# Strassen's up product with one addition fewer, a wider accumulator bank, and a new table of dates

## The chip, the cores and the metric

The kernel runs on one core of a Trainium2 chip. The metric is the device time of one execution in microseconds, median over runs. A core has five engines with instruction streams of their own: PE (TensorE, matrix products; its weight loads are listed apart as PEld), DVE (VectorE), ACT (ScalarE), POOL (GpSimd) and SP (SyncE, which here issues most of the DMA transfers). Operands lie in SBUF; matrix products accumulate in the eight banks of PSUM, 2 KB for each of 128 partitions.

## The reference

```python
def _attn_ref(q, k, v, n_global, n_local):        # B 4, H 8, S 768, D 64; n_global 8, n_local 96
    scores = scale * np.matmul(q, k.transpose(0, 1, 3, 2))
    ...
    keep = is_global | is_local
    ...
    scores = scores + bias[None, :, :, :]          # ALiBi: -slope(head) * distance
    scores = np.where(keep, scores, -1000000000.0)
    ...
    return np.matmul(a, v)                         # a: softmax of scores over the keys

def _moe_ref(x, w_in, w_out):                      # x 3072 x 512, w_in 512 x 2048, w_out 2048 x 512
    h = x @ w_in
    g = h * (1.0 / (1.0 + np.exp(-1.702 * h)))
    return (g @ w_out).astype(np.float32)
```

The rows of the attention's result, all heads side by side, are the 3072 rows `x` of the second function.

## The kernel before

Every fp32 operand is split into two fp16 parts, high and low, and a product is made of three fp16 products. The attention works on 24 blocks of 128 rows (scores `s`, row maxima `NM`, exponentials `p`, values `pv`, result `x`, turned to `xT`). The second part works on 12 chunks `c` of 256 tokens. For each chunk the up product gives 2048 columns of `h`, then `g`, and the down product adds into `y`.

Chunks 0 to 2 use `up` (L861), a plain product. Chunks 3 to 11 use `up_two(c, S)`, S = 0..3, so 36 calls, each for 512 of the 2048 columns. A call is Strassen's algorithm in Winograd's form on 2x2 blocks: seven block products, in the order p1, p5, p6, p3, p2_, p7, p4, each of 12 matmuls of 128x128 (L901), on sums of weights (`T1` to `T4`) and of inputs (`xS`) that were made beforehand. They accumulate in two PSUM tiles, `pa` and `pb`:

- `pa` takes p1; ACT copies that (k1, L917) to `h0`; p6 is added on top, copied (k2, L906) to the other half of `h0`; p7 is added on top; DVE adds that to `h1` (q22); p4 is added on top.
- `pb` holds two sums: p5, copied to `h1` (k5, L906), with p3 on top, and p2_. DVE adds both to the halves of `h0` (q11 and q12, L909).

The sigmoid is made of a tanh: `swish` is one ACT tanh (L933) and one DVE product (L934). For the first half of a call, `h0` (512 wide), it runs once; for the second half it runs twice, over `h1` and over `pa`, 256 wide each. Then `g` is split, its high part on ACT (L941), its low part on DVE (L942), and `down_two` hands each half to `pile` (L969), which issues the down matmuls. For even S `pa` and `pb` are buffers of one ring of PSUM banks (`r_h`), for odd S each has a bank of its own.

The order of all instructions is fixed ahead: each step is a task with a cost, predecessors, buffers and a due time, and `order()` is a list scheduler that, engine by engine, takes the ready task with the earliest due time; the table `NUDGE` adds microseconds to the due times of all tasks with one tag. What comes out is one fixed program order for each engine; on the chip an engine waits for its next instruction and doesn't look past it.

The last tasks are a verdict on whether the fp16 parts hold the inputs: `rows_hold` (DVE), one small PE product `pb` (L1141) that sums over the partitions, `all_hold` (DVE, L1131 to L1137), which writes `flag`. Every engine loads `flag` into a register (L1159) and skips the fallback `general` when it is zero (L1160). Behind the skipped part stand only ACT's scaling of the last quarter of `y` (L994, `junk`) and the DMA of it that ACT issues (L998). ACT's two instructions wait for semaphore counts of DVE, PE and of the DMA queues; engines that skip `general` add to those counts by EVENT_SEMAPHORE instructions at the place they jump to.

Of the kernel before, what the change touches and what calls it, by code (L numbers as in the profile page):

```python
# [8 lines left out]
F32 = mybir.dt.float32  # L9
# [10 lines left out]
P = 128  # L20
# [6 lines left out]

NUDGE = {"M2": -8.8, "T2": 21.9, "T3": 11.2, "block1": 2, "block10u2": -2.7, "block10u2l": -0.5,  # L30
# [36 lines left out]

NG = 8
SKIP = 24
# [54 lines left out]
class Work:  # L124
# [5 lines left out]
    def add(self, on, fn, after=(), bufs=(), want=1e9):  # L130
        t = Task(on, fn, [a for a in after if a is not None], bufs, want)
        t.tag = self.tag + ("l" if "SP" in on else "")
        for a in t.after:
            a.next.append(t)
        for b in t.bufs:
            b.users.append(t)
        self.tasks.append(t)
        return t

    def order(self):  # L140
# [18 lines left out]
        for t in self.tasks:  # L159
            t.due += NUDGE.get(t.tag, 0.0)  # L160
        free = dict.fromkeys(("PE", "DVE", "ACT", "POOL", "SP"), 0.0)
# [84 lines left out]
def kernel(  # L246
# [11 lines left out]
    nc = tc.nc  # L258
# [70 lines left out]
    add = wk.add  # L329
# [68 lines left out]
    M1 = [add({"DVE": 0.61}, lambda e, f=f: slopes(e, slice(2, 3), range(4 * f, 4 * f + 4)), [m1], [mk]) for f in range(2)]  # L398
    wk.tag = "M2"
    m2 = add({"DVE": 0.78}, other, [m1], [flt, mk])  # L400
    M2 = [add({"DVE": 0.41, "ACT": 0.6}, lambda e, f=f: slopes(e, slice(0, 2), range(2 * f, 2 * f + 2)), [m2], [mk], 34.0) for f in range(4)]
# [475 lines left out]
    def up_two(c, S, want):  # L877


        nm = f"{c}_{S}"  # L880
        rx, rz = (r_h, r_h) if S % 2 == 0 else (r_y[1, 0], r_y[1, 1])
        pa, pb = Buf(rx, [P, 2, P], F32, "pa" + nm), Buf(rz, [P, 2, 2, P], F32, "pb" + nm)
        h0, h1 = Buf(r_VF, [P, 2, 2, P], F32, "h0" + nm), Buf(r_VF, [P, 2, P], F32, "h1" + nm)
        ts = [Buf(r_t, [P, 2, 2, P], F32, f"t{nm}_{t}") for t in range(2)]
        gg = [Buf(r_VR if t and c == NCHUNK - 1 else r_g, [P, 2, 2, 2, P], F16, f"g{nm}_{t}") for t in range(2)]
# [2 lines left out]
        half = lambda w, k: (w, lambda z: w()[:, z, 512 * k:512 * k + 512])  # L888
        (B11, B21), B22 = (half(W, 0), half(W, 1)), half(V, 1)
        (T1, T4), (T3, T2) = TT[S, 0], TT[S, 1]  # L890
        a, b, g_ = pa, (lambda: pb()[:, 0]), (lambda: pb()[:, 1])
        wr = [W_ready[2 * S, 0], W_ready[2 * S + 1, 0], x_ready[2 * c], x_ready[2 * c + 1]]
        tr = [*T_ready[S], xS_ready[c]]

# [10 lines left out]
        def keep(o, src, sb_, sp_, after):  # L905
            return add({"ACT": 0.26}, lambda e: nc.scalar.copy(o(), src()), after, [sb_, sp_])  # L906

        def plus(o, src, sb_, sp_, after):
            return add({"DVE": 0.34}, lambda e: nc.vector.tensor_add(o(), src(), o()), after, [sb_, sp_])  # L909

        c11, c12 = (lambda: h0()[:, 0]), (lambda: h0()[:, 1])
        p1 = product(a, B11, X, 0, 0, [*wr, line.get("p1")], pa, 0.0, first=True)
        p1.bufs.append(pb)
# [3 lines left out]
        k1 = add({"ACT": 0.26}, lambda e: nc.scalar.copy(c11(), a()), [p1, line.get("k1")], [h0, h1, pa])  # L917
        line["k1"] = k1
        k5 = keep(h1, b, h1, pb, [p5])
        p6 = product(a, T2, Xs, 0, 0, [*tr, k1], pa, 1.4)  # L920
        p3 = product(b, B22, Xs, 1, 0, [*tr, *wr, k5], pb, 2.1, last=True)
        p2_ = product(g_, B21, X, 1, 0, [*wr, p5], pb, 2.8, last=True)
        q11 = plus(c11, g_, h0, pb, [k1, p2_])
        k2 = keep(c12, a, h0, pa, [p6])
        q12 = plus(c12, b, h0, pb, [k2, p3])
        p7 = product(a, T3, Xs, 0, 1, [*tr, k2], pa, 4.1)
        q22 = plus(h1, a, h1, pa, [p7, k5])
        p4 = product(a, T4, X, 1, 1, [*tr, *wr, q22], pa, 5.5, last=True)
        ups[c, 2 * S] = ups[c, 2 * S + 1] = [p1, p5, p2_, p6, p3, p7, p4]

        def swish(o, src, srcs, after, w):

            t1 = add({"ACT": 0.06 + 0.22 * w}, lambda e: nc.scalar.activation(o(), src(), AF.Tanh, scale=0.851 / (SX * SW)), after, srcs)  # L933
            return add({"DVE": 0.08 + 0.265 * w}, lambda e: nc.vector.scalar_tensor_tensor(o(), o(), 1.0, src(), ALU.add, ALU.mult),  # L934
                       [t1], srcs)

        u0 = [swish(ts[0], h0, [ts[0], h0], [q11, q12], 2)]
        u1 = [swish(lambda: ts[1]()[:, 1], h1, [ts[1], h1], [q22], 1), swish(lambda: ts[1]()[:, 0], a, [ts[1], pa], [p4], 1)]
        for t, u in enumerate((u0, u1)):
            g, tt = gg[t], ts[t]  # L940
            t4 = add({"ACT": 0.53}, lambda e, g=g, tt=tt: nc.scalar.mul(g()[:, 0], tt(), SG / (SX * SW)), u, [tt, g])  # L941
# [76 lines left out]
    T0, PACE0, PACE, PACE2, LAG, SKEW, LEAD = 20.0, 6.0, 5.9, 5.7, 16.0, 3, 68.0  # L1018
# [67 lines left out]
    for s in range(NST):  # L1086
        for u in range(2):
            for half in range(2):
                ws = Buf(r_wa, [P, 512, 2], I32, f"ws{s}_{u}{half}again")
                t0 = add({"SP": 1.6}, lambda e, s=s, u=u, ws=ws, half=half: load_weights(nc, ws(), w_in, w_out, s, u, half), bufs=[ws])  # L1090
                o, hi_w = 2 * (2 * s + u) + half, lambda ws=ws: ws()[:, :, 1].bitcast(F32)
# [16 lines left out]
    pb = Buf(r_h, [P, 512], F32, "pb")  # L1108
# [255 lines left out]
```

## Time and profile before

| | us |
|---|---|
| median of 3 runs | 589.75 |
| the runs | 590.07, 588.32, 589.75 |
| profiled execution, its span | 587.0 |
| PE busy | 578.1 |
| DVE busy | 497.0 |
| ACT busy | 461.4 |

The profile shows one execution by its span, from its first instruction to its last; no other time of that execution is given, so what lies around the span is the 2.75 us between it and the median. "Busy" counts the time in which an engine executes an instruction. An engine's order is fixed, so an idle stretch on PE is a wait for another engine or for a transfer.

### The profile page before, as it was taken

What the parts mean: (1) busy time and instruction counts of PE and PEld (TensorE: products, weight loads), DVE (VectorE), ACT (ScalarE), POOL (GpSimd) and SP (SyncE); (2) the same over time, 40 slices, a digit from 0 to 9 for tenths busy, and PEclk for the clock granted to TensorE, in tenths of its full rate; (3) what the DMA queues carried; (4) which work ended last, traced back from release to release, by engine and by line L of the source; (5) the groups of instructions that cost most, each with busy time, mean ns of one, the idle gap of its engine ahead of it and who ended that gap; (6) DMA issues with size and microseconds to landing.
All of it is one profiled execution on the core that took longest, in us unless ns stands there. A gap on an engine that the chain in (4) does not pass through costs nothing.

```text
span 587.0 us, 16903 instructions
## 1 busy us (share of the span) xinstructions
PE 578.1 (98%) x6744; PEld 435.0 (74%) x6744; DVE 497.0 (85%) x1180; ACT 461.4 (79%) x1086; POOL 3.7 (1%) x14
## 2 busy tenths in 40 slices
PE   8999999999999999999999999999999999999996
PEld 5886666777678678778679767777777866876896
DVE  7898999999999999888899699889889878775462
ACT  6678899898678979888798798798987878874351
POOL 2000000000000000000000000000000000000000
PEclk9999999999999999999999999999999999999999
DMA  9988998988767887989999998999998899981101
GB/s 267 315 262 213 301 239 234 214 186 154 174 138 154 145 150 156 222 163 203 222 182 179 213 222 210 218 201 184 243 204 197 196 204 232 192 179 25 30 2 41
DMA packets 268265, 109.57 MB, mean 187 GB/s; under 512 B 249300, under 2 KB 249812, under 8 KB 268180
## 3 DMA queue, kind: packets, MB, share of 16 engines
q1 hardware_dynamic: 268032, 108.30, 83.3%
q8 instruction: 54, 0.88, 0.6%
q14 instruction: 31, 0.25, 0.1%
q10 hardware_dynamic: 148, 0.13, 0.1%
HBM read 57.67 MB, written 6.29 MB: 109 GB/s over the span
## 4 chain that ended last, share of the span: by engine, by line
PE 82%; DVE 6%; DMA 6%; ACT 4%; issue 2%; SPq 0%; POOL 0%; DVEq 0%; ACTq 0%; POOLq 0%
PE y L969 35%; PE pa L901 15%; PE pb L901 11%; PE h L861 7%; PE s L599 5%; DMA QKover<-qk16over 2%; PE pv L630 1%; PE pv L632 1%; PE pv L631 1%; PE sT L692 1%; DMA ws<-in_moe_w_out_dram 1%; DMA ws_00again<-in_moe_w_in_dram 1%; DMA xT<-x 1%; PE idle L1147 1%; PE pv L704 1%
## 5 line engine op out<-in xcount | busy, mean ns | idle before, releaser
L969 PE MATMUL y<-w,g 128*128 128x512 f16 (+1 forms) x1248 | 265.1, 363 | 0.3
L969 PEld LDWEIGHTS <-g 128*128 128x128 f16 x1248 | 118.0, 98 | 106.6 <-DVE g L873 1.4
L901 PEld LDWEIGHTS <-w 128*128 128x128 f16 x1728 | 101.4, 98 | 3.9
L615 ACT ACTIVATE p<-p,NM 128x232 f32<-128x232 f32 x160 | 76.3, 479 | 8.9 <-DVE NM L605 8.6
L901 PEld LDWEIGHTS <-T 128*128 128x128 f16 x1296 | 76.8, 98 | 5.2 <-issue 0.2
L861 PE MATMUL h<-xT,w 128*128 128x256 f16 x576 | 67.2, 273 | 0.2 <-DVE t L871 0.2
L605 DVE CUSTOM_DVE_ANT_0 p<-s,mm 128x232 f32<-128x232 f32 x160 | 57.5, 393 | 9.3 <-PE s L599 9.0
L861 PEld LDWEIGHTS <-w 128*128 128x128 f16 x576 | 55.4, 98 | 8.1 <-DVE t L871 0.3
L942 DVE SCALAR_TENSOR_TENSOR g<-t,g 128x512 f16<-128x512 f32 x72 | 49.0, 686 | 11.2 <-ACT g L941 10.9
L620 DVE TENSOR_TENSOR hl<-p,hl 128x464 f16<-128x464 f32 x80 | 50.8, 635 | 6.2 <-ACT hl L619 5.9
L941 ACT ACTIVATE g<-t 128x512 f16<-128x512 f32 x72 | 44.9, 628 | 12.1 <-PE y L969 8.2
L933 ACT ACTIVATE t<-h 128x512 f32<-128x512 f32 (+1 forms) x72 | 35.8, 517 | 17.8 <-DVE h L909 16.0
L619 ACT CAST hl<-p 128x464 f16<-128x464 f32 x80 | 46.0, 574 | 2.3 <-DMA pt<-hl 0.9
L909 DVE TENSOR_TENSOR h<-pb,h 128x256 f32<-128x256 f32 x72 | 28.4, 418 | 19.4 <-PE pb L901 17.8
L901 PE MATMUL pa<-xS,T 128*128 128x128 f16 x648 | 44.8, 219 | 0.0
L599 PEld LDWEIGHTS <-QK 128*128 128x128 f16 x640 | 36.5, 98 | 6.0 <-DVE NM L605 1.9
L934 DVE SCALAR_TENSOR_TENSOR t<-t,h 128x512 f32<-128x512 f32 (+1 forms) x72 | 38.4, 551 | 2.2 <-ACT t L933 2.0
L599 PE MATMUL s<-QK 128*128 128x128 f16 x320 | 38.2, 219 | 0.0
L901 PE MATMUL pa<-xT,w 128*128 128x128 f16 x540 | 37.5, 219 | 0.0
L901 PE MATMUL pb<-xS,w 128*128 128x128 f16 x540 | 37.5, 219 | 0.0
L632 PE MATMUL pv<-VR,pt 128*128 128x64 f16 x288 | 34.5, 193 | 0.0
L631 PE MATMUL pv<-VR,pt 128*128 128x64 f16 x288 | 34.5, 193 | 0.0
(186 smaller groups left out, 1031.2 us busy)
## 6 DMA issues: line engine op xcount, KB each, us to landing
ws<-in_moe_w_in_dram SPq DMA_DIRECT2D x8, 1024.0 KB
ws<-in_moe_w_out_dram SPq DMA_DIRECT2D x8, 1024.0 KB, 5.6
raw<-in_q_dram SPq DMA_DIRECT2D x24, 256.0 KB, 3.7
raw<-in_k_dram SPq DMA_DIRECT2D x24, 256.0 KB, 4.8
QK<-QK SPq DMA_DIRECT2D x40, 128.0 KB, 5.5
raw<-in_v_dram SPq DMA_DIRECT2D x20, 256.0 KB, 3.1
out_dram<-yo SPq DMA_DIRECT2D x20, 256.0 KB
ws_00again<-in_moe_w_in_dram SPq DMA_DIRECT2D x8, 512.0 KB, 4.0
```

What stands on the lines that cost most here:

```text
L599: nc.tensor.matmul(sp()[:, j, lo:hi], d["QK"]()[:, 0, h, :], K[:, 1 + z, h, P - (hi - lo):], start=(z == 0), stop=(z == 1), skip_group_che ...
L605: nc.vector.tensor_tensor_reduce(out=pr()[:, j, :], in0=sp()[:, j, :], in1=m, scale=-1.0 / SC, scalar=3.0e38, op0=ALU.add, op1=ALU.min, ac ...
L615: ex.append(add({"ACT": 0.473}, lambda e, j=j: nc.scalar.activation(pr()[:, j, :], pr()[:, j, :], AF.Exp, bias=NM[:, n, hs[j]:hs[j] + 1], ...
L619: t4 = add({"ACT": 0.5}, lambda e: nc.scalar.copy(hl()[:, 0, :, SKIP:], pr()), ex, [pr, hl])
L620: t5 = add({"DVE": 0.55}, lambda e: nc.vector.tensor_sub(hl()[:, 1, :, SKIP:], pr(), hl()[:, 0, :, SKIP:]), [t4], [pr, hl])
L631: nc.tensor.matmul(o, ph, V[:, 1, h], start=False, stop=False, skip_group_check=True)
L632: nc.tensor.matmul(o, pl, V[:, 0, h], start=False, stop=(s == ns - 1), skip_group_check=True)
L861: nc.tensor.matmul(ph()[:, fi, :], w1(s, cc, z, fi), X[:, y, cc, :], start=(j + cc == 0), stop=(j == 2 and cc == NCC - 1))
L901: nc.tensor.matmul(o()[:, fi], w, x()[:, y * NCC + 2 * k + cc, t], start=(first and fi + j + cc == 0), stop=(last and j + cc == 3), skip_g ...
L941: t4 = add({"ACT": 0.53}, lambda e, g=g, tt=tt: nc.scalar.mul(g()[:, 0], tt(), SG / (SX * SW)), u, [tt, g])
L942: t5 = add({"DVE": 0.61}, lambda e, g=g, tt=tt: nc.vector.scalar_tensor_tensor(g()[:, 1], tt(), SG / (SX * SW), g()[:, 0], ALU.mult, ALU.s ...
L969: nc.tensor.matmul(y(), part(zg, f), w2(s, z, f % 2)[:, m], start=(begin and f + j == 0), stop=(end and j == 2 and f == 2 * len(steps) - 1 ...
```

## The change

Four edits in `up_two`, and a new table.

- The tile `pa` is now a whole bank (2 x 256 columns) instead of half of one; products accumulate in its first half. The two halves of `pb` change places, so that they lie in the order of the halves of `h0`.
- q11 and q12, two additions of 256 columns, become one, q1, of 512; it waits for k1, k2, p2_ and p3.
- q22 writes its sum to the second half of `pa`, in PSUM, instead of to `h1`.
- For the second half of a call `swish` runs once, over all 512 columns of `pa`, after p4.
- `NUDGE` is replaced by a table with more entries, among them one for the verdict, which had none. Instructions of PE are the same in number and kind; DVE has 49 fewer, ACT 34 fewer: 36 additions, 36 products and 36 tanh are gone, and some other instructions change places between the two engines.

Lines of the changed kernel are 22 to 27 further on (L901 is L927, L969 is L991, L1141 is L1163, L1160 is L1182).

```diff
-NUDGE = {"M2": -8.8, "T2": 21.9, "T3": 11.2, "block1": 2, "block10u2": -2.7, "block10u2l": -0.5,
...
+         "up92": -40, "up93": -9.5, "verdict": 12.7, "w00": 14.7, "w00l": -2.4, "w01": -6.4, "w01l": -7.8,
...
-        pa, pb = Buf(rx, [P, 2, P], F32, "pa" + nm), Buf(rz, [P, 2, 2, P], F32, "pb" + nm)
+        pa, pb = Buf(rx, [P, 2, 2, P], F32, "pa" + nm), Buf(rz, [P, 2, 2, P], F32, "pb" + nm)
...
-        a, b, g_ = pa, (lambda: pb()[:, 0]), (lambda: pb()[:, 1])
+        a, b, g_ = (lambda: pa()[:, 0]), (lambda: pb()[:, 1]), (lambda: pb()[:, 0])
...
-        def plus(o, src, sb_, sp_, after):
-            return add({"DVE": 0.34}, lambda e: nc.vector.tensor_add(o(), src(), o()), after, [sb_, sp_])
...
-        q11 = plus(c11, g_, h0, pb, [k1, p2_])
         k2 = keep(c12, a, h0, pa, [p6])
-        q12 = plus(c12, b, h0, pb, [k2, p3])
+        q1 = add({"DVE": 0.62}, lambda e: nc.vector.tensor_add(h0(), pb(), h0()), [k1, k2, p2_, p3], [h0, pb])
         p7 = product(a, T3, Xs, 0, 1, [*tr, k2], pa, 4.1)
-        q22 = plus(h1, a, h1, pa, [p7, k5])
+        q22 = add({"DVE": 0.36}, lambda e: nc.vector.tensor_add(pa()[:, 1], a(), h1()), [p7, k5], [h1, pa])
...
-        u0 = [swish(ts[0], h0, [ts[0], h0], [q11, q12], 2)]
-        u1 = [swish(lambda: ts[1]()[:, 1], h1, [ts[1], h1], [q22], 1), swish(lambda: ts[1]()[:, 0], a, [ts[1], pa], [p4], 1)]
+        u0 = [swish(ts[0], h0, [ts[0], h0], [q1], 2)]
+        u1 = [swish(ts[1], pa, [ts[1], pa], [p4], 2)]
```

The instruction orders show the change at three places. The first is DVE in the call of chunk 6, S = 0 (names begin with `t6_0`, `h06_0`, `h16_0`, `pa6_0`), where `x14` and `sm2` belong to the attention of block 14. In the order of before:

```order
L909 TENSOR_TENSOR h16_0_5226<-pa6_0_5000,h16_0_5226 128x256
L942 SCALAR_TENSOR_TENSOR g5_3_1_5265<-t5_3_1_5163,g5_3_1_5265 128x512
L909 TENSOR_TENSOR h06_0_5144<-pb6_0_5130,h06_0_5144 128x256
L934 SCALAR_TENSOR_TENSOR t6_0_1_5324<-t6_0_1_5324,h16_0_5226 128x256
L747 TENSOR_SCALAR sm2_101<-sm2_101 128x8
L748 RECIPROCAL sm2_101<-sm2_101 128x8
L749 TENSOR_TENSOR x14_5354<-pv14_4959,sm2_101 128x512
L934 SCALAR_TENSOR_TENSOR t6_0_0_5350<-t6_0_0_5350,h06_0_5144 128x512
L934 SCALAR_TENSOR_TENSOR t6_0_1_5324<-t6_0_1_5324,pa6_0_5000 128x256
```

In the order of the change (`s15` and `p15` belong to the attention of block 15):

```order
L956 SCALAR_TENSOR_TENSOR t6_0_0_5284<-t6_0_0_5284,h06_0_5148 128x512
L631 ISA p15_2_5286,NM_89<-s15_2_5246,mm_102 128x232
L631 ISA NM_89 128x1
L956 SCALAR_TENSOR_TENSOR t6_0_1_5302<-t6_0_1_5302,pa6_0_5078 128x512
```

The two products of 256 columns for the second half have become one of 512, the last reader of the bank of `pa6_0`. The next call that takes this bank is chunk 6, S = 2. On PE, in the order of the change, these are the first and the last rows from p4 of the one (`pa6_0`) to p1 of the other (`pa6_2`), with the 32 matmuls between them cut to one of each product:

```order
L927 MATMUL pa6_0_5078<-xT6_4558,T0_1891 128x128
...
L927 MATMUL pb6_1_5288<-xS6_4981,T1_2262 128x128
...
L927 MATMUL pb6_1_5288<-xT6_4558,w2_0_581 128x128
...
L625 MATMUL s15_3_5321<-QK15_4775 128x128
...
L927 MATMUL pa6_2_5335<-xT6_4558,w4_0_817 128x128
```

Between them stand two products of 12 matmuls into `pb6_1` and eight score matmuls, the shortest such distance in the change.

The third place is the end of the program. PE in the order of before, where the verdict's product stands ahead of most of the last down products (`y11_00` is the first quarter of the last `y`, `y11_11` the last):

```order
L901 MATMUL pa11_3_9806<-xS11_9345,w5_0_942 128x128
L1141 MATMUL pb_9888<-fin_104,ones_110 1x3
L969 LDWEIGHTS g11_2_0_9775
L969 MATMUL y11_00_9497<-w4_1_846,g11_2_0_9775 128x256
```

and in the order of the change:

```order
L991 MATMUL y11_10_9524<-w7_1_1437,g11_3_1_9840 128x256
L1163 MATMUL pb_9885<-fin_104,ones_110 1x3
L991 LDWEIGHTS g11_1_1_9678
L991 MATMUL y11_11_9554<-w2_1_689,g11_1_1_9678 128x256
```

Behind the product there now stand only the 36 matmuls of `y11_11`. On DVE `all_hold` moves in the same way from ahead of the last five products of `t` and `g` to behind the last `yo`; on SP the load of `flag` moves from ahead of the last four `yo` transfers to behind them. SP before:

```order
L1159 TENSOR_LOAD flag [waits DVE_49]
L1159 ISA x2
L1002 DMA out_dram<-yo_0_9985 64x256 [waits DMAHW2_49,DVE_49]
L1002 DMA out_dram<-yo_0_9985 64x256 [waits DMAHW3_49]
L1002 DMA out_dram<-yo_0_9985 128x256 [waits DMAHW4_49,DVE_49]
L1002 DMA out_dram<-yo_1_10015 128x256 [waits DMAHW5_49,DVE_49]
L1160 COMPARE_AND_BRANCH
```

and in the change:

```order
L1024 DMA out_dram<-yo_0_9855 64x256 [waits DMAHW2_49,DVE_49]
L1024 DMA out_dram<-yo_0_9855 64x256 [waits DMAHW3_49]
L1024 DMA out_dram<-yo_0_9855 128x256 [waits DMAHW4_49,DVE_49]
L1024 DMA out_dram<-yo_1_9899 128x256 [waits DMAHW5_49,DVE_49]
L1181 TENSOR_LOAD flag [waits DVE_49]
L1181 ISA x2
L1182 COMPARE_AND_BRANCH
```

The branch now follows the load with only the two ISA rows between.

## Rows read from the trace of the kernel before

**Rows 1.** The page: span, busy time of each engine with its share of the span and its instructions, and the granted clock of PE in 40 slices (9 is 90% or more of full speed).

```profile
span 587.0 us, 16903 instructions
PE 578.1 (98%) x6744; PEld 435.0 (74%) x6744; DVE 497.0 (85%) x1180; ACT 461.4 (79%) x1086; POOL 3.7 (1%) x14
PEclk9999999999999999999999999999999999999999
```

**Rows 2.** Busy time by stretch: start:end and length in us, then busy us and instructions of PE, PEld, DVE, ACT and POOL, the granted clock, the DMA share and GB/s.

```profile
20.00:60.00 40.00, 38.90 (x329) 31.39 (x328) 35.65 (x59) 30.42 (x41) 0.00 (x0) 1.00 0.90 265
60.00:140.00 80.00, 78.99 (x737) 56.24 (x736) 77.75 (x159) 73.11 (x152) 0.00 (x0) 1.00 0.97 234
140.00:220.00 80.00, 80.00 (x918) 58.10 (x914) 78.04 (x178) 64.41 (x154) 0.00 (x0) 1.00 0.73 147
220.00:300.00 80.00, 80.00 (x1046) 60.19 (x1044) 68.49 (x174) 68.10 (x175) 0.00 (x0) 1.00 0.91 191
420.00:460.00 40.00, 39.86 (x508) 29.43 (x506) 34.01 (x83) 33.77 (x88) 0.00 (x0) 1.00 0.98 200
```

**Rows 3.** Timeline of PE from 402 to 408 us: start, duration of the run from first start to last end, engine, line, operation, names, shapes and count.

```profile
402.36 0.83 PE L901 MATMUL pa<-xT,w 128*128 128x128 f16 x12
403.03 2.75 PE L969 MATMUL y<-w,g 128*128 128x512 f16 x12
...
407.31 0.26 PE L599 MATMUL s<-QKover,QK 128*128 128x104 f16 x2
...
407.71 0.83 PE L901 MATMUL pb<-xS,w 128*128 128x128 f16 x12
```

**Rows 4.** Waits of PE's weight loads over the whole span: line and what it waited for, us in total, times, longest.

```profile
PEld L599 <- DVE NM L605: 1.9, 3, 1.0
PEld L969 <- DVE g L873: 1.4, 3, 0.6
PEld L969 <- DVE g L942: 0.6, 1, 0.6
```

**Rows 5.** Groups of instructions by line and shape: line, engine, operation, output<-inputs, shapes and count, then busy us in all and mean ns of one, then idle time before them. `pa`, `pb` and `pv` lie in PSUM, the rest in SBUF.

```profile
L909 DVE TENSOR_TENSOR h<-pb,h 128x256 f32<-128x256 f32 x72 | 28.4, 418 | 19.4 <-PE pb L901 17.8 <-ACT h L906 0.8 <-ACT p L615 0.4
L934 DVE SCALAR_TENSOR_TENSOR t<-t,h 128x512 f32<-128x512 f32 x36 | 24.6, 684 | 2.2 <-ACT t L933 2.0
L933 ACT ACTIVATE t<-h 128x512 f32<-128x512 f32 x36 | 22.6, 627 | 13.3 <-DVE h L909 12.1 <-DMA out_dram<-yo 1.1
L909 DVE TENSOR_TENSOR h<-pa,h 128x256 f32<-128x256 f32 x36 | 15.0, 418 | 0.8 <-PE pa L901 0.6
L934 DVE SCALAR_TENSOR_TENSOR t<-t,h 128x256 f32<-128x256 f32 x36 | 15.0, 417 | 0.0
L934 DVE SCALAR_TENSOR_TENSOR t<-t,pa 128x256 f32<-128x256 f32 x36 | 14.9, 415 | 5.5 <-ACT t L933 5.5
L933 ACT ACTIVATE t<-h 128x256 f32<-128x256 f32 x36 | 14.6, 407 | 4.5 <-DVE h L909 4.0 <-DVE g L942 0.4
L749 DVE TENSOR_TENSOR x<-pv,sm 128x512 f32<-128x512 f32 x20 | 13.8, 692 | 3.9 <-PE pv L632 1.6 <-DVE sm L748 0.5
L933 ACT ACTIVATE t<-pa 128x256 f32<-128x256 f32 x36 | 13.6, 377 | 7.1 <-PE pa L901 7.1
```

**Rows 6.** Weight loads of `up_two`'s products over the whole span: line, engine, operation and count, then ns shortest/median/longest, then first and last start in us.

```profile
L901 PEld LDWEIGHTS <-w x1728: 95/98/98, 173.8 to 571.8; 128*128 128x128 f16 x192
```

**Rows 7.** The chain that ended last, from 560 us on: start, us, engine, output, line and count.

```profile
569.84 0.12 PE pb L1141 x2
...
572.05 10.49 PE y L969 x96
...
582.62 0.47 ACT junk L994
```

**Rows 8.** Timeline of DVE from 569 us on, columns as in the timeline of PE.

```profile
570.28 0.14 DVE L1131 COPY tot<-pb 1x3 f32<-1x3 f32 x1
...
571.42 0.14 DVE L1137 TENSOR_SCALAR flag<-tot 1x1 int32<-1x1 f32 x1
...
578.64 0.42 DVE L985 TENSOR_SCALAR yo<-y 128x256 f32<-128x256 f32 x1 [0.89 <-PE y L969]
```

**Rows 9.** The instructions of L1159 (load of the flag), L1160 (branch, and the semaphore steps behind it) and L998 (the last DMA): engine queue, operation and count, then ns shortest/median/longest, then first and last start in us.

```profile
L1159 SPq TENSOR_LOAD <-flag x1: 477/477/477, 571.6 to 571.6; - x1
L1159 DVEq TENSOR_LOAD <-flag x1: 542/542/542, 578.6 to 578.6; - x1
L1160 SPq EVENT_SEMAPHORE  x8: 17/17/17, 582.2 to 582.8; - x8
L1160 ACTq COMPARE_BRANCH  x1: 45/45/45, 573.5 to 573.5; - x1
L1160 ACTq EVENT_SEMAPHORE  x1: 17/17/17, 573.9 to 573.9; - x1
L1160 DVEq COMPARE_BRANCH  x1: 72/72/72, 579.3 to 579.3; - x1
L1160 SPq COMPARE_BRANCH  x1: 58/58/58, 579.5 to 579.5; - x1
L1160 DVEq EVENT_SEMAPHORE  x1: 21/21/21, 582.2 to 582.2; - x1
L998 ACTq DMA_DIRECT2D out_dram<-junk x1: 376/376/376, 583.1 to 583.1; - x1
```

More of the change, by code (lines that the diff above doesn't have):

```diff
@@ L26 @@
 LOW = 1e8
-NUDGE = {"M2": -8.8, "T2": 21.9, "T3": 11.2, "block1": 2, "block10u2": -2.7, "block10u2l": -0.5,
[36 rows of a table removed]
+NUDGE = {"M1": -24.1, "M2": -17.9, "T0": -7.8, "T1": 6.4, "T3": 11.6, "again": 14.4, "againl": 1.4,
[62 rows of a table added]
 NG = 8
```

97 rows, old and new, of the table NUDGE are left out of this document.

## The prediction, made before the changed kernel ran

> **What bounds the kernel now.** I read the page first. [...] The share is an average, so the stretches come next [rows 2]. From 140 us on PE is busy 80.00 of 80 us twice, then 39.86 of 40 in the worst of the later ones; DVE in the same stretches is busy 98%, 86% and 85%. There the end is set by PE's work alone. Earlier it is different: from 20 to 60 us PE lacks 1.10 us, from 60 to 140 us 1.01 us, and in the latter DVE is busy 77.75 of 80 us.
>
> Busy PE need not be PE at its best pace, so the timeline has to show the spacing [rows 3]: a product of 12 matmuls starts at 402.36 and the next thing at 403.03, 0.67 us; eight score matmuls take 407.71 - 407.31 = 0.40 us. Seven products take 4.69 us for PE, a call's whole share, and I find that spacing nearly everywhere after 130 us. Last, the waits of PE's weight loads [rows 4]: 1.9 us on the row maxima NM, 1.4 and 0.6 us on the low part of g, all from DVE. These few microseconds, and the end of the program, are all that a change off PE can win or lose.
>
> **What is removed.** A call of `up_two` loses work on two engines and none on PE. On DVE two additions at 418 ns become one of 512 columns [rows 5]. No row has that operation between PSUM and SBUF; the nearest are the normalisation of x, the same operation from PSUM at 512 columns, 692 ns, and the product of 512 columns, 684 ns. With 0.69 us a call saves 0.15 us, 36 calls 5.3 us. The two products of the second half, 417 + 415 ns, become one of 684 ns: 0.15 us, 5.3 us in all. On ACT the tanh of 407 + 377 ns become one of 627 ns: 0.16 us, 5.7 us in all. The times of one instruction overlap a little from one to the next, so DVE gains somewhat less, say 8 us. The first weight load of `up_two` is at 173.8 us [rows 6], so all of it falls behind the stretch in which PE waits; the cover is PE's own full row of work [rows 2], and the 8 us are worth nothing there by themselves.
>
> **What is changed in place.** q22 writes PSUM instead of SBUF. No row shows DVE writing to PSUM. Below, 0 extra: reading `pb` or `pa` instead of SBUF leaves products at 415 beside 417 ns [rows 5]. Above, 0.1 us for each (the 274 ns by which 692 exceeds 418 are twice the columns, not the place, so I find no row for more): 36 x 0.1 = 3.6 us of DVE time, covered from 220 us on by 14% of idle DVE. I take 0.
>
> **What is added: a longer hold on the bank.** Before, q22's half could pass tanh and product while PE did p4; only 377 + 415 ns of work over `pa` remained behind p4. Now all 512 columns wait for p4, 627 + 684 ns, 0.52 us more before the bank is free and before `g` can be split. For the split it matters little: the down products that need this half stand far enough behind p4 in the new order. For the bank it may matter. [...] The shortest distance on PE is that of chunk 6 shown in the change: two products and eight score matmuls, 2 x 0.67 + 0.40 = 1.74 us [rows 3]. Ahead of the last product DVE has there the product for the first half (684 ns) and a row maximum. So this place is at its limit: 0 to 1 us of wait. Counting PE's work in the new order at the same spacings I find two more under 3 us, 2.4 and 2.8. Bounds 0 and 2 us together; I take 0.3, since the nominal chain fits at the shortest place, and most others have over 4 us.
>
> [...]
>
> **New dates, front.** PE's order in the first 54 us is nearly the old one, with a few neighbours exchanged; its waits for ACT and DVE there should stay: 0, with 0.3 either way.
>
> **New dates, 60 to 140 us.** Here DVE is 97% busy and PE waits for it [rows 2]. Laying DVE's work ahead of each wait against PE's, in both orders, at the durations of before, DVE's worst lag behind PE's pace shrinks by 0.5 to 1 us. The waits that could go are those of [rows 4], 1.9 + 1.4 + 0.6 us as weight loads see them, and 1.0 us as PE sees them in 60 to 140 us [rows 2], since loads run ahead of products. I take 0.7 us of gain, bounds 0 and 1.2. In the later stretches PE lacks little, 0.14 us in the row from 420 us; I take 0.1 of gain.
>
> **New dates, the verdict.** This is the largest single term. Before, PE's verdict product stands at 569.84 [rows 7], `all_hold` runs from 570.28 to 571.56 on DVE, 1.28 us [rows 8], and SP loads the flag at 571.6 [rows 9], eleven microseconds ahead of the end of PE at 572.05 + 10.49 = 582.54. Now the product stands ahead of the last 36 matmuls. A down matmul of 256 columns takes 10.49 / 96 = 0.109 us [rows 7], so 36 of them take 3.93 us, and `y11_10` ends at 578.6, as the last `yo` at 578.64 confirms [rows 8]. `yo` ends at 579.0, `all_hold` starts with it done and takes 1.28 us: flag at 580.2 to 580.3. SP's load takes 0.48 us and some register work; I put its branch at 581.0.
>
> What follows the branch decides. On SP the branch is at 579.5 and the eight semaphore steps at its target start at 582.2 and end at 582.8: 2.7 + 0.6 us. On DVE it is at 579.3, the step at 582.2: 2.9 us. On ACT it is 573.5 to 573.9: 0.4 us [rows 9]. With SP's time again: 581.0 + 2.7 + 0.6 = 584.3. With DVE's: load at 580.2, branch 0.7 us later as before, step at 583.8, and then ACT's scaling (474 ns) until 584.3. ACT's last DMA waits for both, and it stands now at 583.1 [rows 9]; nothing hides the difference, since that DMA ends the span 3.9 us later. So +1.2 us. Bounds: 0, if both engines go on as quickly as ACT did (SP 581.0 + 0.4 + 0.6 = 582.0, before PE ends), and +1.5 with the latest reading of each step. I take 1.2: the rows for the two engines in question are the near ones.
>
> [...]
>
> **The sum**, against the span of the profiled execution: 587.0 + 1.2 (verdict) + 0.3 (bank) - 0.7 - 0.1 (waits) = 587.7 us, +0.7. The median of before lies 2.75 us above that span, so 589.75 + 0.7 gives 590.4 us.
>
> **Rivals.**
>
> *The verdict is hidden, and the waits go* (faster). If SP and DVE find the code behind the branch as ACT did, the 1.2 us vanish. Then 0.3 - 0.8 = -0.5 gives 589.2. For it to be faster by more than the measurement can tell, 0.3% or 1.8 us, all 1.2 us of the waits and the 1.1 us that PE lacks in 20 to 60 us must go: -2.3 gives 587.4 us. Against: both engines that matter took nearly 3 us in the trace. Chance of faster than that bound: 0.17.
>
> *The bank is late* (slower). If the first product of a call waits for `pa` at the three short places, and at some others because DVE has an attention row ahead, PE loses 2 us more than I took, and the verdict's 1.2 us remain: 590.4 + 2.0 = 592.4. It decides from the point where the hand-over behind p4 takes over 1.74 us at chunk 6, or over 2.4 us at the next place. [...] Against: most places have over 4 us. Chance 0.15.
>
> *The new dates are worse early.* DVE at 97% has no reserve, so a row maximum put two instructions later (0.7 us each) costs PE as much; three such places are +2 us, again 592.4. Against: the lag that I work out is smaller. Chance 0.06.
>
> *Nothing measurable happens*, the edits lying off the bound and the dates cancelling: my own case, with its 0.7 us unseen.
>
> **How the numbers follow.** My case and its neighbours within 1.8 us of 589.75 have 0.62. Slower by more: 0.15 + 0.06 = 0.21. Faster: 0.17. My own case lies between 589.0 (no verdict term) and 591.4 (the bank at 1.4). For 8 in 10 the range reaches half-way into the rivals: 588.2 to 592.2.
>
> **What would show it.** DVE's busy time should fall to 487 to 490 us and ACT's by some 5 us plus or minus what changes places, with PE's at 578 as before. The 512-column addition should read 0.68 to 0.70 us; q22 0.42. PE's busy share in 60 to 140 us should reach 79.5 of 80. At the end, SP's first semaphore step should stand over 2 us behind its branch, and ACT's DMA over a microsecond behind the end of PE's last product. I am wrong if PE waits for DVE's product over `pa` at chunk 6 or elsewhere by more than 1 us, if ACT's DMA follows PE's end as closely as before (0.6 us), or if DVE's saving reaches PE after all because waits that the trace books as busy PE disappear.

## The result, and the profile after

The changed kernel takes 591.61 us (median of 5 runs, 591.02 to 592.86); the kernel before took 589.74 us in the runs beside it (5 runs, 588.32 to 590.07). The ratio is 1.0054, with a 95% interval of 1.0035 to 1.0074: slower by 3.2 us by the ratio over runs taken in turns; the two medians stand 1.87 us (0.32%) apart, just under the lower end of the interval. The prediction was 590.4 us, no change that a measurement can tell. The time lies inside its range, but the kernel is slower by more than the noise, and that was not forecast.

The profiled execution took 592.86 us with a span of 591.1 us, so 1.76 us lie around the span. In the five runs of the change that figure is 1.75 to 1.9 us. Span and median of before stood 2.75 us apart; the profiled execution of before was therefore about a microsecond quicker than its median, and the 4.1 us between the two spans are more than the difference of the kernels.

The page of the changed kernel, its first lines (as [rows 1]):

```profile
span 591.1 us, 16801 instructions
PE 578.5 (98%) x6744; PEld 435.4 (74%) x6744; DVE 493.3 (83%) x1107; ACT 454.5 (77%) x1051; POOL 3.7 (1%) x14
```

DVE is 3.7 us less busy and ACT 6.9 us, PE is as busy as before in a longer span. Busy time by stretch (as [rows 2]):

```profile
60.00:140.00 80.00, 77.60 (x722) 55.12 (x720) 76.92 (x157) 71.06 (x149) 0.00 (x0) 1.00 0.97 230
...
300.00:380.00 80.00, 78.74 (x1056) 60.05 (x1054) 67.45 (x159) 65.47 (x168) 0.00 (x0) 1.00 0.98 194
```

PE lacks 2.40 us from 60 to 140 us (80.00 less the busy 77.60), where it lacked 1.01, and 1.26 us from 300 to 380 us, where before it lacked nothing in this execution. What PE waited for (engine, line, cause: us, times, longest):

```profile
PE h L887 <- DVE t L897: 1.4, 2, 0.7
PE s L625 <- DVE NM L631: 1.0, 1, 1.0
PE aux L706 <- DVE top L703: 0.9, 1, 0.9
PE pv L656 <- DMA pt<-hl: 0.6, 1, 0.6
PE pa L927 <- ACT h L932: 0.4, 1, 0.4
```

The first two are in the early stretch, the third at 10 us; the last two are those near 312 and 341 us. The joined instructions themselves (columns as in [rows 5]):

```profile
L947 DVE TENSOR_TENSOR h<-pb,h 128x512 f32<-128x512 f32 x36 | 24.7, 686 | 13.1 <-PE pb L927 9.5 <-ACT h L932 3.3
L956 DVE SCALAR_TENSOR_TENSOR t<-t,pa 128x512 f32<-128x512 f32 x36 | 24.5, 681 | 1.8 <-ACT t L955 1.7
L955 ACT ACTIVATE t<-pa 128x512 f32<-128x512 f32 x36 | 21.3, 592 | 13.7 <-PE pa L927 11.6 <-DVE sm L773 2.1
L949 DVE TENSOR_TENSOR pa<-pa,h 128x256 f32<-128x256 f32 x36 | 15.4, 426 | 6.5 <-PE pa L927 6.4
```

The addition of 512 columns takes 686 ns, the one that writes PSUM 426 ns against 418.

The end of the program. PE and then DVE on the timeline (as [rows 8]):

```profile
581.35 0.19 PE L1163 MATMUL pb<-fin,ones 128*1 128x3 f32 x2
581.47 4.10 PE L991 MATMUL y<-w,g 128*128 128x256 f16 x36
...
582.93 0.14 DVE L1159 TENSOR_SCALAR flag<-tot 1x1 int32<-1x1 f32 x1
```

and the flag's load, the branch, the semaphore steps behind it and ACT's last two instructions (as [rows 9]):

```profile
L1181 SPq TENSOR_LOAD <-flag x1: 478/478/478, 583.1 to 583.1; - x1
L1182 SPq EVENT_SEMAPHORE  x8: 17/17/17, 587.4 to 587.9; - x8
L1182 DVEq COMPARE_BRANCH  x1: 72/72/72, 583.7 to 583.7; - x1
L1182 SPq COMPARE_BRANCH  x1: 58/58/58, 584.3 to 584.3; - x1
L1182 DVEq EVENT_SEMAPHORE  x1: 21/21/21, 584.3 to 584.3; - x1
L1016 ACT ACTIVATE junk<-y,room x1: 473/473/473, 585.7 to 585.7; 128x256 f32<-128x256 f32 x1
L1020 ACTq DMA_DIRECT2D out_dram<-junk x1: 376/376/376, 588.1 to 588.1; - x1
```

PE's last product ends at 585.57. ACT's scaling follows at once, at 585.7, but its DMA starts at 588.1, behind SP's eight steps (587.4 to 587.9). Before, the DMA stood 0.6 us behind PE's end, now 2.5. The end of the span moved less: it lies 5.4 us behind the start of ACT's scaling (591.1 and 585.7), before 4.4 (587.0 and 582.62 [rows 7]), because the last transfer ended the span 3.0 us after its issue and not 3.9.

### The profile page after: what moved, and what is told of

It reads as the page before. It is cut to its first block, busy times and chain, and to the rows that moved or that the text cites. A ratio compares the mean times of both kernels' runs of the same rounds, so it can differ in the third digit from the quotient of the medians.

```text
span 591.1 us, 16801 instructions
## 1 busy us (share of the span) xinstructions
PE 578.5 (98%) x6744; PEld 435.4 (74%) x6744; DVE 493.3 (83%) x1107; ACT 454.5 (77%) x1051; POOL 3.7 (1%) x14
## 5 line engine op out<-in xcount | busy, mean ns | idle before, releaser
L991 PE MATMUL y<-w,g 128*128 128x512 f16 (+1 forms) x1248 | 264.3, 363 | 0.0
L991 PEld LDWEIGHTS <-g 128*128 128x128 f16 x1248 | 118.2, 98 | 107.3 <-DVE g L899 0.5
L927 PEld LDWEIGHTS <-w 128*128 128x128 f16 x1728 | 101.1, 98 | 3.4 <-issue 0.3
L927 PEld LDWEIGHTS <-T 128*128 128x128 f16 x1296 | 76.6, 98 | 3.9 <-issue 0.5
L927 PE MATMUL pa<-xS,T 128*128 128x128 f16 x648 | 45.0, 219 | 0.4 <-ACT h L932 0.4
L927 PE MATMUL pb<-xS,w 128*128 128x128 f16 x540 | 37.3, 219 | 0.2 <-ACT h L932 0.2
L927 PE MATMUL pa<-xT,w 128*128 128x128 f16 x540 | 36.8, 219 | 0.0
L947 DVE TENSOR_TENSOR h<-pb,h 128x512 f32<-128x512 f32 x36 | 24.7, 686 | 13.1 <-PE pb L927 9.5
L657 PE MATMUL pv<-VR,pt 128*128 128x64 f16 x288 | 34.8, 193 | 0.0
L658 PE MATMUL pv<-VR,pt 128*128 128x64 f16 x288 | 34.8, 193 | 0.0
L656 PE MATMUL pv<-VR,pt 128*128 128x64 f16 x288 | 34.8, 193 | 0.0
L484 ACT ACTIVATE junk<-raw 128x1024 bf16<-128x1024 f32 (+1 forms) x40 | 33.6, 839 | 0.6 <-issue 0.4
```

The costliest lines, as they stand in the source:

```text
L656: nc.tensor.matmul(o, ph, V[:, 0, h], start=(s == 0), stop=False, skip_group_check=True)
L657: nc.tensor.matmul(o, ph, V[:, 1, h], start=False, stop=False, skip_group_check=True)
L927: nc.tensor.matmul(o()[:, fi], w, x()[:, y * NCC + 2 * k + cc, t], start=(first and fi + j + cc == 0), stop=(last and j + cc == 3), skip_g ...
L991: nc.tensor.matmul(y(), part(zg, f), w2(s, z, f % 2)[:, m], start=(begin and f + j == 0), stop=(end and j == 2 and f == 2 * len(steps) - 1 ...
```

## The experiments

Each is given as a ratio to the kernel before, timed on the same chip in turns with it. Theory 1 is that the late verdict costs, theory 2 that PE's waits from the new dates cost, theory 3 that the edits themselves cost, by the longer hold on the bank of `pa`. Two more came up on the way.

**The verdict of the change, dated earlier.**

```diff
-         "verdict": 12.7,
+         "verdict": 4,
```

> The changed kernel with its verdict dated 8.7 us earlier, so that the flag is written and SP loads it ahead of the last yo transfers; all else as in the change. If the late verdict is a cost (theory 1): ACT's last DMA follows PE's last product by 0.6 us again instead of 2.5, the time falls by 1.0 to 2.0 us, to 589.6 to 590.6. If the cost is only PE's waits from 60 to 380 us (theory 2): within 0.4 us of 591.6.

Measured: 589.59 us beside 588.11 of before, ratio 1.0023 (1.0012 to 1.0033). Against 1.0054 this is 0.31%, 1.8 us; by the two intervals it can be 0.5 to 3.1 us. In its trace, the chain's last pieces, then SP's branch and steps and ACT's DMA:

```profile
574.97 10.17 PE y L991 x93
...
585.21 0.47 ACT junk L1016
```

```profile
L1182 SPq EVENT_SEMAPHORE  x8: 17/17/17, 585.0 to 585.5; - x8
L1182 SPq COMPARE_BRANCH  x1: 58/58/58, 582.4 to 582.4; - x1
L1020 ACTq DMA_DIRECT2D out_dram<-junk x1: 376/376/376, 585.7 to 585.7; - x1
```

SP's branch comes 2.8 us ahead of ACT's scaling and its steps are through in time; the DMA stands 0.6 us behind PE's end again. The span ends 4.0 us behind the start of the scaling, 1.4 us less than in the change. The late verdict is a cost, theory 1 holds for it, but 0.23% are left. The same kernel was run once more on another chip:

> The changed kernel with the early verdict once more, beside the two others on one chip: 1.0012 to 1.0033 of before, as the first time.

Measured: 589.52 beside 587.89, ratio 1.0023 (1.0013 to 1.0033).

**The verdict of before, dated later.**

```diff
-         "x9l": 1.9}
+         "x9l": 1.9, "verdict": 20}
```

> The kernel before with its verdict dated 20 us later, so that the flag is written behind the last yo; all else as before. Theory 1: ACT's last DMA stands 2 to 2.5 us behind PE's end, the time rises by 1.0 to 2.0 us, to 590.8 to 591.7. Theory 2: 589.7, unchanged within 0.4.

Measured: 591.41 us, ratio 1.0058 (1.0044 to 1.0073), 3.4 us, more than any theory had. Here both engines are slow behind the branch:

```profile
L1160 SPq EVENT_SEMAPHORE  x8: 17/17/17, 585.0 to 585.6; - x8
L1160 DVEq COMPARE_BRANCH  x1: 72/72/72, 581.2 to 581.2; - x1
L1160 SPq COMPARE_BRANCH  x1: 58/58/58, 581.4 to 581.4; - x1
L1160 DVEq EVENT_SEMAPHORE  x1: 21/21/21, 585.0 to 585.0; - x1
L998 ACTq DMA_DIRECT2D out_dram<-junk x1: 376/376/376, 585.7 to 585.7; - x1
```

DVE takes 3.8 us and SP 3.6, and since DVE is late ACT's scaling is late too (585.1, with PE done at 581.7).

**The edits with the dates of before.** The body of the change, the old table; the order is made anew.

```diff
-NUDGE = {"M1": -24.1, "M2": -17.9, "T0": -7.8, ...
+NUDGE = {"M2": -8.8, "T2": 21.9, "T3": 11.2, ...
```

> The four edits in up_two alone, with the dates of before (the verdict early). If the edits cost nothing (theories 1 and 2): 589.2 to 590.2, PE's waits ahead of 140 us as before. If the longer hold on the bank of pa costs (theory 3): 591 or more, with PE waits for DVE's product over pa or for ACT's tanh in 220 to 560 us.

Measured: 591.39 us, ratio 1.0053 (1.0040 to 1.0067). By its expectation that speaks for theory 3, but the trace shows another cause. ACT, then PE, near 306 us:

```profile
305.30 0.68 ACT L1088 ACTIVATE ws_00again<-ws_00again 128x512 f32<-128x512 f32 x1 [2.88 <-DMA ws_00again<-in_moe_w_in_dram]
...
307.52 0.37 ACT L906 COPY h<-pa 128x256 f32<-128x256 f32 x1
```

```profile
307.94 0.83 PE L901 MATMUL pa<-xS,w 128*128 128x128 f16 x12 [1.28 <-ACT h L906]
```

ACT stands 2.88 us at a check of reloaded weights, whose transfer is late. In the order made with the old dates this check stands ahead of the copy that PE's next product needs; in the trace of before the copy stands at 304.78, ahead of the same check. PE has other waits in this execution: 0.9 us for transposed p, 0.7 us for values, 0.5 us for a copy that had too little work between itself and the next product. None is for the product or the tanh over `pa`.

**The dates of the change with the old body.** The new table in the kernel before.

```diff
-NUDGE = {"M2": -8.8, "T2": 21.9, "T3": 11.2, ...
+NUDGE = {"M1": -24.1, "M2": -17.9, "T0": -7.8, ...
```

> The table of the change alone, with up_two as before. If the dates are the whole difference (theories 1 and 2): 591.2 to 592.4, with PE losing about 1.5 us at the row maxima near 72 us and at the up products near 107 and 111 us, and the late verdict's tail. If the edits in up_two are the difference (theory 3): 589.3 to 590.3.

Measured: 602.05 us, ratio 1.0235 (1.0216 to 1.0255). Neither theory has this. PE's largest waits:

```profile
PE pa L927 <- ACT h L943: 3.1, 2, 2.3
PE pb L927 <- DVE xS L823: 1.5, 1, 1.5
```

Copies and sums come too late for PE, as in the run before this; what holds each of them up was not followed further. In the early stretch the trace has the wait of the change: 1.4 us for `t` (L897), here with the old body. A table and a body belong together; neither alone is a measure of what it adds to the other. Here, besides, ACT jumps slowly and SP quickly:

```profile
L1186 SPq EVENT_SEMAPHORE  x8: 17/17/17, 590.4 to 590.9; - x8
L1186 ACTq COMPARE_BRANCH  x1: 50/50/50, 589.5 to 589.5; - x1
L1186 SPq COMPARE_BRANCH  x1: 58/58/58, 589.8 to 589.8; - x1
L1186 ACTq EVENT_SEMAPHORE  x1: 17/17/17, 592.8 to 592.8; - x1
```

**Theory 4: ACT's wait for the reloads.** Three kernels in exactly the orders of before, of the edits with old dates, and of the change with the early verdict; only the operand of the 32 checks is another, and with it the places that they write.

```diff
-                o, hi_w = 2 * (2 * s + u) + half, lambda ws=ws: ws()[:, :, 1].bitcast(F32)
+                o, hi_w = 2 * (2 * s + u) + half, lambda: idle
...
```

> The kernel before, in its own order, but the 32 checks of the reloaded weights (ACT square, DVE minimum) read a tile that is always there instead of the one that the DMA brings; the reloads stay, the check of the weights' range is left out. If ACT's wait for these reloads is what the edits made costly (theory 4), before has little of it: 0 to 0.4 us under before (587.7 to 588.1 on this chip). A rival, that the reloads' traffic or the checks' work cost by themselves, would also give no change here; it is told apart by the next run.

> The four edits with the dates of before, in the same order as in body_only, with the checks reading the resident tile as in the run before this. Theory 4: ACT no longer stands 2.9 us at the reload near 302 us, PE's wait of 1.4 us for a copy near 306 us is gone, the time falls by 1.2 to 2.2 us from 591.4. Rival (the edits' longer chain on the bank and on ACT costs, theory 3): within 0.5 us of 591.4. Waits of PE for transposed p and for VR (0.9 and 0.7 us) may stay in either.

> The changed kernel with the early verdict, in the same order, with the checks reading the resident tile. Theory 4: PE's waits near 341 to 379 us, 1.2 to 2 us, go or halve; the time falls by 0.6 to 1.5 us from 589.6. Rival (theory 3): within 0.4 us of 589.6.

Measured: before 589.40 us beside 588.82, ratio 1.0006 (0.9991 to 1.0020), no change; the edits with old dates 590.81, 1.0039 (1.0023 to 1.0056), 0.14% under the 1.0053 of that kernel; the change with the early verdict 590.88, 1.0042 (1.0026 to 1.0057), over its 1.0023. Neither difference is clear of the intervals. In the traces the wait at 306 us is gone, and PE's waits behind 150 us are few: in the change with the early verdict a single one of 0.2 us, in the edits with old dates these:

```profile
PE pv L630 <- DMA VR<-VG: 0.8, 1, 0.8
PE pa L901 <- ACT h L906: 0.5, 1, 0.5
```

But the times didn't follow as forecast. The program's end hides a part. With the edits and old dates ACT's scaling starts at 584.5 and not 586.3, 1.7 us earlier, and then the last transfer takes 1.0 us of that back: it ends the span 4.3 us after its issue and not 3.3. In the change with the early verdict it takes 4.7 us where it took 3.5 and 3.4. These are single executions. So the mechanism at 306 us is seen, its worth in the time is not settled; for the change as it is, theory 4 isn't borne out.

**Theory 5: the edits in the old order.** The joined instructions stand where the later of the two stood, nothing is scheduled anew.

```diff
+        joined.append((q11, q12, lambda e: nc.vector.tensor_add(h0(), pb(), h0()), None))
...
-        for t in wk.order():
+        seq_ = wk.order()
+        when = {t: i for i, t in enumerate(seq_)}
+        for x, z, fn, made in joined:
+            first_, last_ = sorted((x, z), key=lambda t: when[t])
+            first_.fn, last_.fn = (lambda e, made=made: made and made()), fn
+        for t in seq_:
```

> The four edits of up_two set into the order of before, without a new schedule: PE and SP have exactly the rows of before, on DVE and ACT the joined addition, tanh and product stand at the later place of the two that they replace and nothing else moves. If the edits themselves are harmless and it is the order made anew around them that lost time in body_only (theory 5): within 0.6 us of before. If the longer hold on the bank and the later split of g cost (theory 3): 1.5 us or more over before, with PE waiting for DVE's product over pa. DVE 5 to 9 us less busy in either.

Measured: 588.11 us beside 587.89, ratio 1.0002 (0.9993 to 1.0011). A line of its page, and the early stretch:

```profile
PE 578.0 (99%) x6744; PEld 435.0 (74%) x6744; DVE 492.9 (84%) x1108; ACT 457.5 (78%) x1050; POOL 3.7 (1%) x14
```

```profile
60.00:140.00 80.00, 78.96 (x740) 56.25 (x738) 77.86 (x158) 73.09 (x154) 0.00 (x0) 1.00 0.98 236
```

DVE is 4.1 us less busy than before (5 to 9 were expected), ACT 3.9 us, and the time is the same. From 300 to 380 us PE lacks nothing. The edits are neither a gain nor a loss; theory 3 falls.

**The change's front, two ways.** First, the dates of chunks 0 to 3 from before, the later ones from the change (for the up and down products, chunks 0 to 2):

```diff
-         "block4u1": -40, ... "up14": 28.7, ... "w70": 24.8, ... "w71": 6.8, ...
+         "block4u1": -10.1, ... "w70": 24.7, ...
```

> The edits with the early verdict; the dates of everything that belongs to chunks 0 to 3 are those of before, the later ones those of the change. If the change's early dates cost what the trace shows (the first aux product 0.5, row maxima near 72 us 0.4, up products near 107 and 111 us 1.4 us), PE's excess ahead of 140 us falls from 9.0 to 7.8 us, and the time by 1.0 to 1.4 us from 589.6, if the later order doesn't lose anew.

Measured: 598.54 us, ratio 1.0183 (1.0158 to 1.0208); the later order lost anew, with 1.4 us of PE at one wait for transposed p near 310 us and 1.0 at one for ACT. The time tells nothing of the front. The trace does: with the old early dates the wait for `t` is 0.2 us again and that for `aux` 0.4. Second, eight tasks moved by hand in the fixed order, PE's and SP's orders left as they are:

```diff
+        ahead(at("block4u0", "DVE", 0), at("w50", "DVE", 1))
+        ahead(at("block4u0", "DVE", 1), at("w50", "DVE", 1))
+        ahead(at("up15", "ACT", 0), at("w71", "ACT", 0))
+        ahead(at("up15", "DVE", 0), at("w71", "DVE", 1))
...
+        ahead(at("up14", "DVE", 0), at("w71", "DVE", 2))
```

> The changed kernel with the early verdict, and eight tasks of DVE and ACT moved ahead of a weight's split near 71 and 103 to 108 us (the row maxima of block 4, the tanh and product of two up chunks); PE and SP keep their order. If the new early dates cost what the trace shows, PE's waits at 72.6 us (0.6 to 1.2) and at 107 and 111 us (0.9 and 0.8) go and the time falls by 1.5 to 2.3 us under after_verdict_early. If such a wait only hides another behind it: by less than 0.5 us.

Measured: 590.54 us, ratio 1.0038 (1.0025 to 1.0052), beside 1.0023 (1.0013 to 1.0033) of the same kernel without the moves on the same chip: no gain, and by the intervals no certain loss. Busy time from 60 to 120 us without the moves, then with them, and PE's waits from 60 to 140 us with them:

```profile
60.00:120.00 60.00, 58.37 (x528) 40.86 (x526) 57.95 (x115) 54.54 (x111) 0.00 (x0) 1.00 0.97 241
```

```profile
60.00:120.00 60.00, 58.17 (x522) 40.05 (x520) 57.46 (x112) 53.62 (x109) 0.00 (x0) 1.00 0.96 240
```

```profile
PE s L625 <- DVE NM L631: 1.2, 2, 0.8
PE y L991 <- DVE g L899: 0.3, 1, 0.3
PE h L887 <- DVE t L897: 0.2, 1, 0.2
```

The waits for t at 107 and 111 us shrank from 1.4 to 0.2 us, and others for DVE took their place: PE lacks 1.83 us in these 60 us instead of 1.63, and 2.02 us in the other execution without the moves. DVE is busy 97% of the stretch without them and 96% with them. With these eight moves the waits changed place, and their sum stayed between those of the two executions without them.

## Why the prediction was right or wrong, point by point

**What bounds the kernel: right.** PE's own work sets the time, at a granted clock of 0.999 of full speed in the profiled executions of before and of the change. The edits in the old order took 4 us from DVE and 4 us from ACT and nothing from the time.

**The edits: right in effect, the saving over-stated.** DVE's busy time fell by 3.7 us to 493.3, not by some 8 to between 487 and 490. The single durations were as estimated (686, 681 and 426 ns), but two short instructions behind each other already overlapped: products of 256 columns start 0.33 us apart (before, at 301.36, 301.69 and 302.02), instructions of 512 columns 0.60 us (the change with the early verdict, 376.05 and 376.65). That leaves 0.06 us for a pair and 4.3 us for 72 pairs, by these spacings; the edits in the old order gave 4.1 us. In the change three more casts on DVE and other exchanges with ACT took some of it back. The wait for the bank of `pa` at chunk 6 didn't come: no trace lists a wait of PE for the product over `pa`. The 0.3 us that the sum has for it were my estimate, and no run shows them: in the change p4 of that call ends at 320.78 us, its tanh runs from 320.81 to 321.41, its product from 321.50 to 322.18, 1.40 us behind p4, and the next p1 on the bank starts at 322.36, straight behind the score matmuls. The second rival is refuted by the sign that the forecast named for it.

**The new dates from 60 to 140 us: wrong, in sign.** Forecast 0.7 us of gain; PE's idle time there rose from 1.01 us [rows 2] to 2.40 us in the profiled execution, and without the late verdict it was 2.02 and 1.63 us; the busy 79.5 of 80 us that the forecast named came in no trace. The step that failed is the comparison of DVE's work ahead of each wait with PE's: it gave a lag smaller by 0.5 to 1 us, and the traces show a larger one. PE waits 1.4 us for `t` in all five traces that have the new early dates without the moves, the old body's among them, and 0.2 us in all seven that have the old ones; it lacks 1.63 to 2.40 us from 60 to 140 us with the new early dates, 0.85 to 1.62 us with the old. The place at 111 us shows how. DVE in the change, then before:

```profile
108.35 2.36 DVE L452 SCALAR_TENSOR_TENSOR w<-wa,w 128x1024 f16<-128x1024 f32 x2 [0.20 <-ACT w L451]
...
111.23 0.68 DVE L897 SCALAR_TENSOR_TENSOR t<-t,h 128x512 f32<-128x512 f32 x1
```

```profile
108.52 0.68 DVE L871 SCALAR_TENSOR_TENSOR t<-t,h 128x512 f32<-128x512 f32 x1
109.11 1.22 DVE L426 SCALAR_TENSOR_TENSOR w<-wa,w 128x1024 f16<-128x1024 f32 x1
```

Both halves of a weight's split (L452) now stand ahead of the product `t` that PE needs; before, the second half stood behind it. In the same way the row maxima of block 4 went from 69.84 us, ahead of a split, to 73.27 us, behind one: that is the third rival's mechanism. Moved ahead of the splits, the waits for `t` fell to 0.2 us, but others took their place, with DVE at 96%. Late transfers add to it and don't explain it: ACT stands 1.9 us for values, but 1.5 us before too, and with the early verdict, in the execution in which DVE doesn't wait for keys, PE still waits 1.4 us for `t`. The early product `aux` waited 0.9 us where it had waited 0.4; PE's busy time in the first 20 us fell from 17.95 to 17.72 us, inside the 0.3 either way that I gave the front.

**The later waits: wrong, but small.** I forecast 0.1 us of gain. The profiled execution lost 1.26 us from 300 to 380 us; one of the two executions with the early verdict lost 1.42 us there, the other nothing. It goes with late transfers: in that stretch ACT stands 4.7 and 4.9 us for reloaded weights in the two that lost, 1.1 us in the one that didn't. How much of the median this makes isn't settled. In the change ACT didn't look past one of these checks: the sum that the tanh behind it needs is ready at 306.37 us, the check starts at 306.70, after 1.28 us of idle time, and the tanh at 307.38.

**The verdict: right in direction, its steps mis-sized.** Forecast 1.2 us; moved back, it is worth 0.31%, 1.8 us, with 1.2 well inside the uncertainty. In the trace the last DMA stands 1.9 us further behind PE's end. Four terms differ. SP's branch comes 1.2 us behind the flag's load, not 0.75: with no transfers between them the register work after the load (583.6 to 584.3) is exposed. The way from branch to first step is 3.1 us, not 2.7. And DVE, which I also took to be slow, jumped in 0.6 us; ACT's scaling was in time, and SP alone decided. Last, I held that nothing hides the difference, since the last DMA ends the span 3.9 us after its issue; in the change it took 3.0 us, so that of the 1.9 us the span shows 1.0 against before, and 1.4 and 1.5 against the two executions with the early verdict. Taking SP's row and not ACT's was right; that the term came near was in part luck, since a longer way to the DMA and a shorter last transfer offset each other.

In these traces the way from the branch falls in two ranges: on DVE, ACT and SP the first step stands either 0.5 to 0.6 us or 2.3 to 3.8 us behind it, over the same skipped code, and which engine is slow changes with the program (DVE 2.9 and 0.6, SP 3.1 and 0.5, ACT 0.5 and 3.4). The profile also lists transfers of instructions, on the queues q8 (16 KB each) and q14 (8 KB each). In the change, between SP's branch and its first step, from 584.3 to 587.4 us (queue: transfers, MB, share):

```profile
q14 instruction: 4, 0.03, 3.6%
q8 instruction: 1, 0.02, 1.9%
```

In all 13 traces at least two such transfers run from start to end inside each of the 18 slow intervals of DVE, ACT and SP (before, three inside DVE's 2.9 us and inside SP's 2.7; in the change, five inside SP's 3.1), and none inside a quick one. Which engine a transfer serves isn't in the trace, so that an engine waits for one is not shown.

**The sum.** By the ratios, 3.2 us are 1.8 of verdict and 1.4 of the order made anew (0.23%, measured alike on two chips), which in the traces is PE's waits; the edits themselves are nothing. I had 1.2 for the verdict and 0.3 - 0.8 = -0.5 for bank and waits. The sum went wrong by the waits, 1.9 us, more than by the verdict, 0.6 us. The 2.75 us from span to median were about 1 us too many for that execution, which shifts the absolute time forecast and not the difference.

**The rivals.** The slower cases that I named, the bank and a front that costs 2 us, had 0.21 between them. The first didn't happen. The second, the front, which had 0.06, did in kind, with about 1.4 us in place of 2, and with the verdict on top that was enough.

## What to carry to other kernels

Shorter instructions on an engine off the bound were worth nothing here, and re-dating the list schedule around them cost more than they could give: put an edit into the old order first, as a measurement of its own. Work at the very end of a program that decides a branch should be through well ahead of the last product, since in these traces the first step behind the branch came up to 3.8 us late, on an engine that another program's trace shows as quick. Where one engine is busy 96% of a stretch, look at the sum of its waits before moving single ones: here they changed place.

## What the hardware showed unexpectedly

The last transfer, 128 KB from ACT's queue (q10), ended the span 3.0 to 4.7 us after its issue: 3.9 before, 3.0 after, 3.5 with the early verdict, 4.7 in the kernel with the other operand of the checks. It goes with a transfer of instructions. Before, from 583.1 to 585.4 us:

```profile
q10 hardware_dynamic: 144, 0.13, 17.9%
q8 instruction: 1, 0.02, 3.0%
```

The 16 KB of q8 run from 583.51 to 584.59 us, the 144 packets of the last transfer from 583.99 to 585.29 us, 1.3 us. In the change q8 is through at 586.88, and the packets take 0.5 us (588.94 to 589.46). In all 13 traces they take 0.5 us in the four in which q8 is through ahead of them and 0.7 to 1.9 us in the nine in which it still runs when they start. No run moves q8 alone, so it is not shown that it is the cause. A verdict written late thus got a quicker last transfer with its delay.

The addition that writes PSUM instead of SBUF cost 426 ns against 418.
